# Fifteen whole output stores issued from SyncE's queue instead of ScalarE's, in a pruned-weight matrix product

## The chip, the cores and the metric

The kernel runs on one core of one Trainium2 chip. The metric is device microseconds (us) of one execution; the time before is 233.33 us, the median of three runs that lay between 233.15 and 233.38 us.

## What is computed

The reference takes x (16 x 512 x 1024, so 8192 rows of 1024 numbers in bf16), a weight w (1024 x 1024) and a bias b (1024). In every column of w, each group of four neighbouring rows keeps its two numbers of largest magnitude and the others become zero. The output is x times the pruned weight plus the bias.

```
wg = w.reshape(G, M, D)                    # M = 4, G = 256
mag = jnp.abs(wg)
order = jnp.argsort(mag, 1)
thr = jnp.take_along_axis(mag, order[:, M - N:M - N + 1, :], 1)     # N = 2
mask = mag >= thr
wp = (wg * mask).reshape(D, D)
return jnp.einsum("bsd,df->bsf", x, wp) + b
```

## The kernel before

The 8192 rows are cut into 64 tiles of 128 rows (`NT = 64`, tiles 0 to 63). One tile needs sixteen matrix products: eight blocks of 128 along the inner dimension (`KT = 8`) by two halves of 512 output columns (`FH = 512`). TensorE wants x with the inner dimension on the partitions, so x has to come transposed.

The work has two stages. In the first, the weight is loaded, pruned on VectorE and spread into `wp_nat`, while the first tiles are begun with what is there; its order is written out by hand, engine by engine, in `order` (line 258). Nothing of it is touched here. It is over when the tiles of `closes` (line 389) are done: tiles 0 to 11.

The second stage is the loop at line 437 over seven batches of tiles: tiles 12 to 15, and then six batches of eight, 16 to 23, 24 to 31, 32 to 39, 40 to 47, 48 to 55 and 56 to 63. A batch of x is brought by one transposing DMA, `load_nat` (line 374, the DMA at line 377), into a buffer `xb`, of which there are two (line 56). It is issued from SyncE's queue, SP. At the head of batch `bi` the program issues the load of batch `bi + 1` (line 439). With two buffers, that load may start when TensorE is through with batch `bi - 1`, and its data are needed when TensorE comes to batch `bi + 1`. So one load waits on SP for the last product of a batch and has the time of the next batch to land.

For each tile, TensorE makes its sixteen products into two banks `ps` of PSUM (`psum_o` has six, line 59); VectorE adds the bias to each half and writes it to `o` (`evac`, line 398, the instruction at line 400); and one DMA of 256 KB stores `o` to the output (`store`, line 411, which goes through `issue`, line 96). There are ten buffers `o` (line 57), so the buffer of one tile is written again ten tiles later.

A DMA is issued by an engine's queue: SP, which does no arithmetic, or ScalarE's queue, ACTq. ScalarE itself has nothing to compute in the second stage. Each queue works in the order in which the program issues, which `seq` (line 64) pins: an issue that waits holds up everything behind it in its queue. Within a batch the program order is: the load of the next batch, and then the eight stores.

From tile 59 on (`LATE = 5`), each tile is stored by halves, all from ACTq. The last tile, 63, is cut into four pieces, whose stores are issued in turn from SP and ACTq (line 449). Thus in the program before, SP issues nothing between the load of tiles 56 to 63 and the first piece of tile 63.

Of the kernel before, what the change touches and what calls it, by code (L numbers as in the profile page):

```python
# [10 lines left out]
def kernel(  # L11
# [20 lines left out]
    NT = NTOK // P  # L32
# [63 lines left out]
    def issue(eng, out_, in_):  # L96
        q = nc.sync if eng == "sp" else nc.scalar
        return seq(eng, q.dma_start(out_, in_))  # L98
# [138 lines left out]
    def nat(xt, ps, c0, c1, k0=0, k1=KT, first=0, last=KT - 1, koff=0):  # L237
        for kt in range(k0, k1):
            pe(nc.tensor.matmul(ps, lhsT=xt[:, kt - koff, :], rhs=wp_nat[:, kt, c0:c1],  # L239
                                start=(kt == first), stop=(kt == last)))  # L240
# [139 lines left out]
    def load_batch(bi):  # L380
        if bi < len(batches):
            tb, nb = batches[bi]
            xnat.update(load_nat(tb, tb + nb))
# [14 lines left out]
    def evac(o, ps, c0, c1, add=None):  # L398
        if add is None:
            dve(nc.vector.tensor_tensor(o[:, c0:c1], ps, bias_sb[:, c0:c1], op=Alu.add))  # L400
        else:
            dve(nc.vector.tensor_tensor(o[:, c0:c1].rearrange("p (n c) -> p n c", n=2),  # L402
                                        ps.rearrange("p (n c) -> p n c", n=2), add, op=Alu.add))

    def rows(t):
        if t < NPK:
            ov, n = tokens(of, t)
            return ov[:, n, :]
        return of[t * P:(t + 1) * P, :]

    def store(eng, t, o, c0=0, c1=Dout):
        issue(eng, rows(t)[:, c0:c1], o[:, c0:c1])
# [24 lines left out]
    for bi, (tb, nb) in enumerate(batches):  # L437
        if bi:
            load_batch(bi + 1)
        for j in range(nb):  # L440
            t = tb + j
            xt = xnat[t]
            o = outp.tile([P, Dout], bf16, name="o")
            if t == NT - 1:
                for n, (c0, c1) in enumerate(((0, FH), (FH, FH + CW), (FH + CW, Dout - P), (Dout - P, Dout))):
                    ps = psum_o.tile([P, FH], fp32, name="ps")
                    nat(xt, ps[:, :c1 - c0], c0, c1)
                    evac(o, ps[:, :c1 - c0], c0, c1)
                    store("act" if n % 2 else "sp", t, o, c0, c1)
            else:  # L450
                pss = [psum_o.tile([P, FH], fp32, name="ps") for _ in range(2)]
                for kt in range(KT):
                    for h in range(2):
                        nat(xt, pss[h][:], h * FH, (h + 1) * FH, kt, kt + 1)
                for h in range(2):
                    evac(o, pss[h][:], h * FH, (h + 1) * FH)
                    if t >= NT - LATE:
                        store("act", t, o, h * FH, (h + 1) * FH)
                if t < NT - LATE:
                    store("act", t, o)  # L460


# [28 lines left out]
```

## Time and profile before

| what | value |
|---|---|
| time, median of three runs | 233.33 us |
| time of the profiled execution | 233.28 us |
| its span, first to last instruction | 231.5 us |
| TensorE clock granted, mean | 1.000 |
| VectorE busy (L400 and L402 among it) | 108.1 us, 47% |
| ScalarE busy | 13.7 us, 6% |
| one load of eight tiles, at line 377, from issue to landing, median | 13.9 us |
| one store of 256 KB from ACTq, from issue to landing, median | 2.6 us |

The span is what the profile covers; 1.78 us of the profiled execution's time lie around it. Lines of the profile name an engine (PE is TensorE, DVE is VectorE, ACT is ScalarE, SP is SyncE; a q behind a name is that engine's queue of issues), a line of the kernel, and what is written from what: `o<-ps,bias_sb` is a tile `o` written from `ps` and `bias_sb`. A wait reads "waiter <- what it waited for". Where a DMA is issued, the duration is that of the issuing instruction on its queue; the time to landing is given separately.

### The profile page before, as it was taken

The numbers are of one execution on the slowest core, as the hardware profiler recorded it, in microseconds if no ns is written. First come the engines' busy times: TensorE is split into PE (matmuls) and PEld (weight loads), VectorE is DVE, ScalarE is ACT, GpSimd is POOL, SyncE is SP. The second block draws the span as 40 slices with busy tenths as digits, with TensorE's granted clock in tenths as the row PEclk, the third lists the DMA queues.
The fourth block names the chain that finished last, engine by engine and source line by source line (L and its number), as shares of the span: only waits on it lengthen the run. The fifth ranks groups of instructions, "written<-read, shape, count | busy, mean of one in ns | idle before, by whom it ended". The sixth has DMA issues, their size and how long they took to land.

```text
span 231.5 us, 2851 instructions
## 1 busy us (share of the span) xinstructions
PE 227.7 (98%) x1158; PEld 112.4 (49%) x1158; DVE 108.1 (47%) x188; ACT 13.7 (6%) x27; POOL 17.6 (8%) x15
## 2 busy tenths in 40 slices
PE   8999999999999999999999999999999999999995
PEld 4887444544444444444444444444444444444443
DVE  4999878854334324324424424424424423433434
ACT  3674100000000000000000000000000000000000
POOL 1000199700000000000000000000000000000000
PEclk9999999999999999999999999999999999999999
DMA  6989989996399221993259921695229952122122
GB/s 184 348 221 224 224 180 259 305 226 242 136 213 269 106 93 62 216 238 123 88 114 221 254 93 61 170 268 159 72 91 189 224 176 83 56 91 86 57 87 91
DMA packets 78268, 38.19 MB, mean 165 GB/s; under 512 B 63664, under 2 KB 70576, under 8 KB 78256
## 3 DMA queue, kind: packets, MB, share of 16 engines
q1 hardware_dynamic: 67328, 20.61, 44.3%
q10 hardware_dynamic: 10928, 17.40, 21.8%
q8 instruction: 9, 0.15, 0.3%
q14 instruction: 3, 0.02, 0.0%
HBM read 3.41 MB, written 16.78 MB: 87 GB/s over the span
## 4 chain that ended last, share of the span: by engine, by line
PE 96%; DVE 1%; DMA 1%; ACTq 0%; issue 0%
PE ps L239 88%; PE ps L216 6%; PE tp L239 1%; DMA w_sb<-in_w_dram 1%; PE tp L189 1%; DVE hi L154 0%; DVE lo L154 0%; DVE mag L154 0%; ACTq L98 0%; DVE mag L164 0%; DVE o L400 0%; DVE wp L154 0%
## 5 line engine op out<-in xcount | busy, mean ns | idle before, releaser
L239 PE MATMUL ps<-wp_nat,xb 128*128 128x512 bf16 (+2 forms) x848 | 179.8, 375 | 0.0
L239 PEld LDWEIGHTS <-xb 128*128 128x128 bf16 x848 | 82.4, 98 | 97.5
L400 DVE TENSOR_TENSOR o<-ps,bias_sb 128x512 bf16<-128x512 f32 (+1 forms) x112 | 71.6, 677 | 113.9 <-PE ps L239 113.8
L396 POOL TENSOR_TENSOR st<-st,bias_sb 128x1024 f32<-128x1024 f32 x8 | 16.7, 2131 | 0.0
L216 PE MATMUL ps<-wp,xt 128*128 128x256 bf16 x128 | 15.1, 273 | 0.1
L239 PE MATMUL ps<-wp_nat,xlow 128*128 128x512 bf16 x64 | 14.1, 379 | 0.0
L216 PEld LDWEIGHTS <-xt 128*128 128x128 bf16 x128 | 12.3, 98 | 1.7 <-ACT xt L194 0.2
L402 DVE TENSOR_TENSOR o<-ps,st 128x512 bf16<-128x512 f32 x16 | 11.1, 692 | 2.8 <-PE ps L239 2.3
L239 PE MATMUL ps<-wp_nat,xlead 128*128 128x512 bf16 x48 | 11.2, 379 | 0.0
L239 PEld LDWEIGHTS <-xlow 128*128 128x128 bf16 x64 | 7.2, 112 | 6.7
L239 PEld LDWEIGHTS <-xlead 128*128 128x128 bf16 x64 | 6.2, 98 | 7.1
L256 ACT COPY st<-ps 128x512 f32<-128x512 f32 x16 | 8.4, 595 | 6.5 <-PE ps L216 3.7
L154 DVE TENSOR_TENSOR mag<-mag,hi 128x256 bf16<-128x256 bf16 (+3 forms) x10 | 5.6, 583 | 0.2
L154 DVE TENSOR_TENSOR wp<-w_sb,mag 128x256 bf16<-128x256 bf16 (+3 forms) x10 | 5.6, 582 | 0.1
L133 PE MATMUL ps<-const-bfloat16-1.0 128*128 128x128 bf16 (+1 forms) x22 | 4.0, 364 | 0.8 <-PEq L475 0.8
L164 DVE TENSOR_SCALAR mag<-w_sb 128x512 uint16<-128x512 uint16 (+2 forms) x6 | 2.7, 469 | 3.2 <-DMA w_sb<-in_w_dram 3.2
L239 PE MATMUL tp<-wp_nat,xlead 128*128 128x512 bf16 x16 | 4.1, 379 | 0.0
L133 PEld LDWEIGHTS <-const-bfloat16-1.0 128*128 128x128 bf16 x22 | 2.2, 131 | 2.4 <-issue 2.4
L154 DVE TENSOR_TENSOR hi<-mag 128x512 bf16<-128x512 bf16 (+2 forms) x7 | 3.2, 459 | 0.1
L189 PE MATMUL tp<-ident,x 128*128 128x128 bf16 x32 | 3.0, 221 | 0.3 <-ACT xt L194 0.2
L154 DVE TENSOR_TENSOR lo<-mag 128x512 bf16<-128x512 bf16 (+2 forms) x7 | 3.2, 457 | 0.0
L194 ACT COPY xt<-tp 128x256 f32<-128x256 f32 x8 | 2.9, 374 | 3.2 <-PE tp L189 3.2
(15 smaller groups left out, 13.4 us busy)
## 6 DMA issues: line engine op xcount, KB each, us to landing
out_dram<-o ACTq DMA_DIRECT2D x59, 256.0 KB, 2.6
wp_nat<-wp SPq DMA_DIRECT2D x14, 128.0 KB, 3.5
w_sb<-in_w_dram SPq DMA_DIRECT2D x3, 512.0 KB, 7.0
out_dram<-o ACTq DMA_DIRECT2D x8, 128.0 KB, 1.7
x<-in_x_dram SPq DMA_DIRECT2D x2, 256.0 KB, 4.1
w_sb<-in_w_dram SPq DMA_DIRECT2D x1, 256.0 KB, 5.1
x<-in_x_dram ACTq DMA_DIRECT2D x1, 256.0 KB, 4.3
bias_sb<-in_b_dram SPq DMA_DIRECT2D x1, 256.0 KB, 7.1
```

Of the source, the lines that this page charges most:

```text
L133: pe(nc.tensor.matmul(warm_ps[:, :rep * P], lhsT=nc.const_aps.tensor(1.0, [P, P], bf16), rhs=nc.const_aps.tensor(1.0, [P, rep * P], bf16), ...
L154: dve(nc.vector.tensor_tensor(out, a, b_, op=op))
L164: dve(nc.vector.tensor_single_scalar(self.mag[:, ms, :].bitcast(u16), self.w[:, ms, :].bitcast(u16), 0x7FFF, op=Alu.bitwise_and))
L189: pe(nc.tensor.transpose(tp[:, m, :], xg[:, m, :], ident[:]))
L194: act(nc.scalar.copy(xt[:].bitcast(fp32), xpk[t].bitcast(fp32)))
L216: pe(nc.tensor.matmul(ps[:, c0 + d:c1 + d], lhsT=xpk[t][:, m, :], rhs=wp[:, g, m, c0:c1], start=(new and m == ms.start), stop=(left[(q, n) ...
L239: pe(nc.tensor.matmul(ps, lhsT=xt[:, kt - koff, :], rhs=wp_nat[:, kt, c0:c1], start=(kt == first), stop=(kt == last)))
L256: act(nc.scalar.copy(st[:, n % 2, :, :].rearrange("p t c -> p (t c)"), ps_open.pop((q, n))[:]))
L396: pool(nc.gpsimd.tensor_tensor(st[:], st[:], bias[:, :, None, :].to_broadcast([P, 2, 2, CW]), op=Alu.add))
L400: dve(nc.vector.tensor_tensor(o[:, c0:c1], ps, bias_sb[:, c0:c1], op=Alu.add))
L402: dve(nc.vector.tensor_tensor(o[:, c0:c1].rearrange("p (n c) -> p n c", n=2), ps.rearrange("p (n c) -> p n c", n=2), add, op=Alu.add))
```

## The change

The whole stores of the odd tiles from 29 to 57, fifteen in number, are issued from SP instead of ACTq. `NT - 36` is 28, and `NT - LATE` is 59. The even tiles, the tiles before 28, the half stores from tile 59 on and the pieces of tile 63 stay where they are, and no data, buffer or loop is changed.

```
                     if t >= NT - LATE:
                         store("act", t, o, h * FH, (h + 1) * FH)
                 if t < NT - LATE:
-                    store("act", t, o)
+                    store("sp" if t >= NT - 36 and t % 2 else "act", t, o)
```

Two of the moved stores (29 and 31) fall in the batch 24 to 31; four each fall in the batches 32 to 39, 40 to 47 and 48 to 55; one (57) falls in the last batch. The last tiles of these batches (31, 39, 47, 55) are odd, so the stores of 31, 39 and 47 stand on SP directly ahead of a load; behind that of 55 no load is left.

More of the change, by code (lines that the diff above doesn't have):

```diff
@@ L459 @@
                 if t < NT - LATE:
-                    store("act", t, o)
+                    store("sp" if t >= NT - 36 and t % 2 else "act", t, o)
 _INS = ['x', 'w', 'b']
```

## The prediction

> **What bounds the kernel now.** I read the page's busy time first, then the chain of waits, and then, because the edit touches only queues, the waits of SP's queue, the pace of VectorE and the issues and landings of the loads.
>
> ```profile
> PE 227.7 (98%) x1158; PEld 112.4 (49%) x1158; DVE 108.1 (47%) x188; ACT 13.7 (6%) x27; POOL 17.6 (8%) x15
> PE 96%; DVE 1%; DMA 1%; ACTq 0%; issue 0%
> ```
>
> ```profile
> 37.97 190.85 PE ps L239 x900
> 228.82 0.02 issue
> 228.85 0.29 DVE o L400
> ```
>
> The first line is the busy time: TensorE works 98% of the span. The others are the chain that ended last: from 37.97 us it is TensorE's products alone, 190.85 us without a step to another engine, then 0.29 us of VectorE's last addition. No store, no load and no queue appears in it in the part of the program that the edit touches, which begins with tile 29. So the time changes only if something makes TensorE wait after about 110 us, or if the 2.4 us behind the last addition (229.14 to 231.5) change.
>
> The timeline of VectorE gives TensorE's pace, since each pair of additions starts when TensorE has ended a tile:
>
> ```profile
> 118.08 1.29 DVE L400 TENSOR_TENSOR o<-ps,bias_sb 128x512 bf16<-128x512 f32 x2 [2.17 <-PE ps L239]
> 121.54 1.29 DVE L400 TENSOR_TENSOR o<-ps,bias_sb 128x512 bf16<-128x512 f32 x2 [2.16 <-PE ps L239]
> 124.99 1.29 DVE L400 TENSOR_TENSOR o<-ps,bias_sb 128x512 bf16<-128x512 f32 x2 [2.17 <-PE ps L239]
> ...
> 145.71 1.29 DVE L400 TENSOR_TENSOR o<-ps,bias_sb 128x512 bf16<-128x512 f32 x2 [2.16 <-PE ps L239]
> ```
>
> A tile takes 3.45 us (121.54 - 118.08 = 3.46; over eight tiles, (145.71 - 118.08) / 8 = 3.454). The first of these rows is tile 31: the load behind it starts 0.21 us later. The last is tile 39. A batch lasts 27.6 us.
>
> **SP before.** The issues of the three loads that will have moved stores ahead of them (the timeline of SP's queue), and what SP waits for:
>
> ```profile
> 118.29 9.85 SPq L377 DMA_TRANSPOSE xb<-in_x_dram  x1
> ...
> 145.92 8.81 SPq L377 DMA_TRANSPOSE xb<-in_x_dram  x1
> ...
> 173.55 10.07 SPq L377 DMA_TRANSPOSE xb<-in_x_dram  x1
> ```
>
> ```profile
> SPq L377 <- PE ps L239: 116.8, 5, 28.7
> SPq L98 <- DMA out_dram<-o: 33.6, 1, 33.6
> SPq L98 <- DVE o L400: 11.0, 2, 10.5
> ```
>
> Issuing a load occupies SP for about 10 us, and the rest of a batch (some 17 us) SP waits for TensorE. The load at 118.29 brings tiles 40 to 47, needed when tile 39 ends, at 145.71. The second wait shows that an issue waits for older DMAs too: the first piece of tile 63 waited 33.6 us, from the end of the load's issue (173.55 + 10.07 = 183.62) to 217.2, which is when the first half of tile 59 had landed, eight issues earlier (its addition began at 214.78 and took 0.69, the store 1.7 us).
>
> ```profile
> out_dram<-o ACTq DMA_DIRECT2D x59, 256.0 KB, 2.6
> xb<-in_x_dram SPq DMA_TRANSPOSE x7, 13.9
> out_dram<-o SPq DMA_DIRECT2D x1, 128.0 KB, 1.8
> ```
>
> These are issues with the time to landing. The three loads above, taken one by one, landed in 13.9, 13.1 and 14.0 us; the longest of all seven took 17.4.
>
> **The change, part by part.**
>
> *Off ACTq:* fifteen issues of 0.338 us (median of the 69 output stores there), 5.1 us of a queue that stands on no chain and whose engine computes nothing after 36 us. Worth nothing: TensorE's products cover it.
>
> *Onto SP, ahead of a load.* Before, the load at 118.29 went out 0.21 us after TensorE's last product of the batch. Now the store of tile 31 stands ahead of it and waits for VectorE: 118.08 + 1.29 = 119.37. Then come 0.03 us to the issue (SP's last-tile store went out at 227.80, its addition having ended at 227.08 + 0.69 = 227.77), 0.36 us for the issue (SP's two output stores took 344 and 368 ns), and some 0.05 us to the next. The load goes out at 119.8, **1.5 us late**. A whole store from SP is not in the trace; SP's copies took 0.34 to 1.57 us to issue, so the delay lies between 1.5 and 2.7 us. Should the load's packets also have to wait until the store has landed (up to 2.9 us, the median of the stores beside the load at 90.67), it is 5.6 at most; at least it is 1.3 (SP's waits gone, the store's issue at nothing). I take 1.5, because the nearest rows are SP's own output stores. This happens to three loads, 4.6 us in all, and costs nothing while each lands in time: 119.8 + 13.9 = 133.7 against 145.7, **12.0 us to spare**; the third, 175.1 + 14.0 = 189.1 against 200.96, leaves 11.9. At the worst of all bounds, 118.29 + 5.6 + 17.4 = 141.3, it is still 4.4 us early. Without that cover each late load would cost its delay.
>
> *Onto SP, behind a load.* The additions of tile 33 end at 124.99 + 1.29 = 126.28, but SP is then issuing the load until 119.8 + 9.85 = 129.65; this store goes out 3.4 us later than from ACTq. The other odd stores of the batch come after 129.65 and do not wait for SP. How long a store takes to land behind a transpose is bounded by 1.8 us (the SP store at the end, with nothing in front) and 17.4 us (as slow as the slowest load). The spreads of the weight on the same queue are near rows: four copies issued right behind the two transposes of `xlead` landed in 3.0 us, four in front of them in 3.9, so I take 3 us: tile 33 has landed by 132.7, at the latest by 147.1. Its buffer `o` is written again by tile 43, at 124.99 + 10 x 3.454 = 159.5, so 12 us remain even at the bound. The DMA eight issues later, which may wait for it, is the store of tile 40, at 149.16 + 1.29 = 150.5, and nothing on TensorE's side waits for that in turn for another ten tiles. The sum over this part is nothing; the work that hides it is ten tiles of products, 34.5 us.
>
> The page "DMA: Bandwidth & Descriptors" of the Trainium skill (section "Queues, rings and completion order") says that each DMA engine takes up the descriptors of one queue in the order they were put there, and that SP and ScalarE have a queue each. It speaks against the change: on SP the store of tile 33 would have to stand behind a whole batch of transposes, on ACTq it need not. By that rule the store lands only near the load's own end, about 134 us; by the copies of `wp_nat` in the trace at about 133; the total is the same by both, as 159.5 is far off.
>
> *The end.* Tile 57's additions end near 209.2 (207.87 + 1.29), SP is free then (the store of tile 55 goes out near 202.3), and its next issue, the first piece of tile 63, is at 227.80: eighteen us lie between. The last issue of all, from ACTq at 229.2, follows the last addition by 0.06 us. Nothing of it changes.
>
> **Sum.** 231.5 us of span + 0, and 1.78 us around it: 233.28, where the three runs have a median of 233.33. I predict **233.3 us**. The runs spread by 0.1%, and 0.2% (0.47 us) is about what this kernel's measurement can tell from no change.
>
> **The rivals.**
>
> *A load comes late (slower).* The loads and their stores now share one ordered queue, and mixing copies into transposes could stretch a load: its stretch of the trace is already full (DMA share 1.10 and 208 GB/s from 90.7 to 104.6 us, 0.26 and 96 GB/s in the rest of the batch). The place is the first product of tiles 40, 48 and 56. It decides once a load takes longer than 27.4 - 1.5 = 25.9 us to land, 1.9 times the 13.9 seen. At twice its time (27.8) it costs 1.9 us a batch, three times: 5.7, or 239.0 us. Against it: copies and transposes already alternate on SP between 10 and 35 us, and none there took over 17.4. Chance 0.05.
>
> *TensorE's pace falls a little (slower).* The edit puts other packets next to the products; 0.25% of the 118 us behind tile 29 is 0.3, 0.4% is 0.5: 233.8. Against it: the tile takes 3.45 us in the crowded half of a batch and in the quiet half alike. With other unseen fixed costs of this size, 0.10.
>
> *The tail gets shorter (faster).* Fewer issues on ACTq could let the end close sooner. SP's waits for the last stores sum to 1.4 us in the closing; half of that gone gives 232.6. Against it: the last eight stores from ACTq are the same ones, 3.45 us apart by pairs, and each lands in about 1.7. Chance 0.08.
>
> *The edit does not move what it says.* The condition holds for 15 tiles and SP can issue plain stores (two are in the trace); the time would be the same 233.3. It is counted with no change.
>
> **How the numbers follow.** No change: 0.77, faster 0.08, slower 0.15. The unknown costs all stay under their cover, so the likeliest case has its own range of 232.9 to 233.8. To leave out under 2 in 10, I stretch it to 232.7 and 234.3, which takes in part of the tail and the pace cases; the late load lies outside.
>
> **What would show it.** Section 6 should list 44 whole stores from ACTq and 15 from SP. The loads near 118.3, 145.9 and 173.6 should go out 1.5 us later, land in 13 to 17 us, and SP should wait for VectorE instead of TensorE there. The store of tile 33 should go out near 129.7. TensorE's pieces in the chain should stay unbroken from 38 to 228.8 us. The prediction is wrong if TensorE's chain breaks at tile 40, 48 or 56 for a DMA into `xb`, if VectorE waits for a DMA out of `o`, or if the span behind the last addition is not 2.4 us.

## The result, and the profile after

The changed kernel takes 233.77 us (median of 22 runs, 233.48 to 234.31), the kernel before, run beside it, 233.37 us (22 runs, 233.01 to 233.67). The ratio is 1.0017 with a 95% interval of 1.0011 to 1.0023: a loss of 0.4 us, small but clear of the spread. The profiled execution took 234.01 us, its span 232.2.

On the two queues the profile is as the prediction said, except that the loads land sooner than its 13 to 17 us. First the page's DMA issues of the kernel after (times to landing last), with the loads' line from its view of DMA queues:

```profile
out_dram<-o ACTq DMA_DIRECT2D x44, 256.0 KB, 2.8
out_dram<-o SPq DMA_DIRECT2D x15, 256.0 KB, 2.0
...
xb<-in_x_dram SPq DMA_TRANSPOSE x7, 11.2
```

Fifteen whole stores are on SP, and the median load lands sooner than before (11.2 against 13.9 us), not later. The timeline of SP's queue after the change, and VectorE's at the end of tile 31:

```profile
118.36 1.29 DVE L400 TENSOR_TENSOR o<-ps,bias_sb 128x512 bf16<-128x512 f32 x2 [2.17 <-PE ps L239]
```

```profile
112.77 7.24 SPq L98 DMA_DIRECT2D out_dram<-o  x2
120.11 8.54 SPq L377 DMA_TRANSPOSE xb<-in_x_dram  x1
128.74 18.90 SPq L98 DMA_DIRECT2D out_dram<-o  x4
147.73 8.98 SPq L377 DMA_TRANSPOSE xb<-in_x_dram  x1
```

The load goes out 1.75 us after tile 31's additions begin; before it was 0.21 (118.29 - 118.08). It is 1.54 us late. The end of the chain of waits shows that this costs nothing:

```profile
38.25 190.85 PE ps L239 x900
229.10 0.02 issue
229.13 0.29 DVE o L400
```

TensorE's last stretch is 190.85 us long, to the digit what it was. It begins 0.28 us later because this one execution was that late already near 10 us, long before any moved store: the chain's long piece of the first stage, 11.35 us on PE, begins at 10.06 us instead of 9.78. Three of the four other kernels below that lose time begin it between 9.77 and 9.85 us. So of the 0.75 us between the two spans, 0.28 belong to the start of this execution, and the rest stands behind the last addition. That stretch lasted 229.14 to 231.47 us, 2.33 us, before, and lasts 229.42 to 232.22, **2.80 us**, now.

The view of DMA from 227 us to the end, of the kernel before and of the kernel after (for queues: packets, MB, share of the 16 engines; for issues: size and time to landing):

```profile
out_dram<-o SPq DMA_DIRECT2D x1, 128.0 KB, 1.8
out_dram<-o ACTq DMA_DIRECT2D x1, 64.0 KB, 1.6
out_dram<-o SPq DMA_DIRECT2D x1, 32.0 KB, 1.5
out_dram<-o ACTq DMA_DIRECT2D x1, 32.0 KB, 1.5
```

```profile
q14 instruction: 1, 0.01, 0.5%
...
out_dram<-o SPq DMA_DIRECT2D x1, 128.0 KB, 1.7
out_dram<-o ACTq DMA_DIRECT2D x1, 64.0 KB, 2.3
out_dram<-o SPq DMA_DIRECT2D x1, 32.0 KB, 2.2
out_dram<-o ACTq DMA_DIRECT2D x1, 32.0 KB, 1.9
```

The last three pieces of tile 63 land 0.4 to 0.7 us later, and one packet is there that was not there before: a load of instructions, `q14 instruction`. In the trace it has 8192 bytes, starts at 229.78 us, 0.36 us behind the last addition, and takes 0.46 us. The page's list of queues says the same of the whole span: `q14 instruction` went from 3 packets to 4.

One more reading ties the packet to the stores. A store completes in sixteen parts, whose completions the trace records one by one. In us behind the last addition, for the very last piece (32 KB from ACTq), the first and the three last of the sixteen:

```
              first   14th   15th   16th
before         1.34   1.46   1.47   1.49
after          1.34   1.47   1.49   1.96
```

Fifteen parts land as before; one is 0.47 us late, as much as the tail (the stretch behind the last addition) is longer (2.80 - 2.33). Of each of the two pieces before it, too, one part of sixteen lands 0.6 to 0.7 us behind the other fifteen. The core has sixteen DMA engines; the trace does not name the one that carried the code load, but one part of sixteen held up is what one occupied engine would do. (The packets of `n14` below show it more closely.) SP's closing waits show where it is paid:

```profile
SPq L486 <- DMA out_dram<-o: 1.4, 4, 0.4
```

```profile
SPq L486 <- DMA out_dram<-o: 1.5, 2, 1.1
```

These are the waits at the end of the program, before and then after (sum, number, longest): the longest went from 0.4 to 1.1 us.

### The profile page after: what moved, and what is told of

The parts are those of the page before. It is cut to its first block, busy times and chain, and to the rows that moved or that the text cites. A ratio compares the mean times of both kernels' runs of the same rounds, so it can differ in the third digit from the quotient of the medians.

```text
span 232.2 us, 2851 instructions
## 1 busy us (share of the span) xinstructions
PE 228.3 (98%) x1158; PEld 113.0 (49%) x1158; DVE 108.0 (47%) x188; ACT 13.8 (6%) x27; POOL 17.6 (8%) x15
## 4 chain that ended last, share of the span: by engine, by line
PE 98%; DVE 0%; issue 0%
PE ps L239 88%; PE ps L216 6%; PE ps L133 2%; PE tp L239 1%; PE tp L189 1%; DVE o L400 0%
## 5 line engine op out<-in xcount | busy, mean ns | idle before, releaser
L239 PE MATMUL ps<-wp_nat,xlead 128*128 128x512 bf16 x48 | 11.2, 379 | 0.0
L189 PE MATMUL tp<-ident,x 128*128 128x128 bf16 x32 | 3.6, 252 | 0.0
(15 smaller groups left out, 13.9 us busy)
```

The costliest lines, as they stand in the source:

```text
L189: pe(nc.tensor.transpose(tp[:, m, :], xg[:, m, :], ident[:]))
```

## The experiments

Why is there a code load more? Each moved store puts two instructions on SP's queue, its issue and a wait for an older DMA, so SP has 90 instructions in the trace instead of 60. The theory (A): a queue fetches its code (its instructions) in blocks; SP comes to the end of one at about its 81st instruction, which now falls into the closing of the program. The rival (B): a store on SP's queue costs something by itself, through the loads it shares the queue with or through the pieces of tile 63 behind it. Theory A makes the loss depend only on how many instructions SP has and on when it comes to that one. Eight kernels were run, each 10 to 12 times, beside the kernel before.

**No store moved, thirty empty instructions on SP**

```
                     store("act", t, o)
+                    if t >= NT - 36 and t % 2:
+                        for _ in range(2):
+                            sp(nc.sync.drain())
```

> The kernel before, all stores from ACTq, with 30 empty instructions (drains) added to SP's queue in pairs behind the odd tiles 29 to 57; no DMA is moved. Theory A (a code load of 8 KB, started when SP comes to about its 81st instruction, falls among the last stores): SP has 90 instructions as after the change, so a code load of 8192 bytes appears 0.3 to 0.4 us behind the last addition, the last stores land 0.4 to 0.7 us later, the stretch from the last addition to the end of the span is 2.8 us instead of 2.33, and the time is 233.8, ratio 1.0017. Theory B (stores on SP's queue cost something by themselves, by sharing it with the loads or with the last pieces): no store is on SP, so 233.37 and a tail of 2.33 us.

Measured: 233.95 us, ratio 1.0020 (1.0011 to 1.0029). The view of DMA from 227 us on:

```profile
q14 instruction: 1, 0.01, 0.7%
...
out_dram<-o ACTq DMA_DIRECT2D x1, 64.0 KB, 2.5
out_dram<-o SPq DMA_DIRECT2D x1, 32.0 KB, 2.3
out_dram<-o ACTq DMA_DIRECT2D x1, 32.0 KB, 2.1
```

The whole loss without one moved DMA. The code load starts at 229.72, 0.26 us behind the last addition, and the tail is 2.94 us.

**Ten, twenty, and fifteen other stores moved**

```
-                    store("sp" if t >= NT - 36 and t % 2 else "act", t, o)
+                    store("sp" if t >= NT - 26 and t % 2 else "act", t, o)   # n10
+                    store("sp" if t >= 19 and t % 2 else "act", t, o)        # n20
+                    store("sp" if t <= 41 and t % 2 else "act", t, o)        # early15
```

> Ten stores moved instead of fifteen (odd tiles 39 to 57). Theory A: SP ends with 80 instructions, so no code load falls in the tail, which is 2.33 us; 233.4, ratio 1.000. Theory B: two thirds of the loss, 233.64, ratio 1.0011, with a tail between.

Measured: 233.36 us, ratio 1.000, with a wide interval (0.9983 to 1.0016; one of the twelve runs took 235.48 us); the tail is 2.39 us. By the time alone B's 1.0011 isn't excluded; by the trace the code load starts at 232.24, when the span is over, and the last three pieces land in 1.6, 1.5 and 1.5 us, as before.

> Twenty stores moved (odd tiles 19 to 57). Theory A: SP has 100 instructions and comes to its 81st some ten instructions earlier, at 185 to 200 us, so the code load stands in the middle of a batch where nothing waits for it; tail 2.33 us, 233.4, ratio 1.000. Theory B: four thirds of the loss, 233.9, ratio 1.0023.

Measured: 233.37 us, ratio 0.9997 (0.9987 to 1.0007); the code load starts at 186.3 and the tail is 2.33 us. More stores on SP than the change has, and no loss: B falls.

> Fifteen stores moved, but those of the odd tiles 13 to 41. Theory A: the number of SP's instructions is that of the change, so the code load is again in the tail: 2.8 us, 233.8, ratio 1.0017. Theory B in the form that the late stores or loads are to blame: nothing is moved behind tile 41, the tail is 2.33 us and the time 233.4.

Measured: 233.92 us, ratio 1.0021 (1.0012 to 1.0031); the code load starts at 229.48, and the tail is 2.69 us. So here it does not matter which stores are moved, late ones or early ones. This execution's last addition ended at 229.19, so it has the loss without the late start of the profiled execution above.

**One store fewer, one store more.** The trace of `n20` narrowed the place: the code load came while SP's 80th instruction still waited, 1.46 us after the 79th (184.84). In the changed kernel the 79th is at 228.46, 1.32 us ahead of its code load.

```
+                    store("sp" if t >= 31 and t % 2 else "act", t, o)        # n14
+                    store("sp" if t >= 27 and t % 2 else "act", t, o)        # n16
```

> Fourteen stores moved (odd tiles 31 to 57). In the runs so far the code load started 1.1 to 1.5 us after SP's 79th instruction. Theory A with that: here the 79th is the first wait of the closing, about 0.25 us behind the last issue from SP, so the code load starts 1.2 to 1.4 us behind the last addition, when the last pieces' data are being written or just have been: loss between 0 and 0.2 us, ratio 1.000 to 1.001, tail 2.33 to 2.5 us. Theory B (a cost per store on SP): 14/15 of the loss, ratio 1.0016.

Measured: 234.12 us (233.1 to 234.93), ratio 1.0032 (1.0018 to 1.0046), worse than the change. Here the expectation failed in size: it gave a loss of 0.2 us at most and a tail of 2.5. Three of the twelve runs, at 233.10 to 233.42 us, show no loss; their traces are not on record. The view of DMA from 227 us on:

```profile
q14 instruction: 1, 0.01, 0.6%
...
out_dram<-o ACTq DMA_DIRECT2D x1, 64.0 KB, 1.6
out_dram<-o SPq DMA_DIRECT2D x1, 32.0 KB, 1.5
out_dram<-o ACTq DMA_DIRECT2D x1, 32.0 KB, 2.3
```

The code load started at 230.19, earlier than reckoned (1.06 us behind the last addition and 1.1 behind the 79th instruction), and met the last piece alone. The trace has each packet: the last piece goes out as sixteen groups of nine packets. The packets of fifteen groups go out between 0.88 and 1.14 us behind the last addition; the nine of the sixteenth start at 1.64, where the code load ends (1.063 + 0.576 = 1.639). So one group stood behind the code load. Fifteen of its parts landed by 1.55, the sixteenth at 2.28; the tail is 3.12 us. That part is 0.79 us late, more than the 0.58 us of the code load; what the remaining 0.2 us are is not shown.

> Sixteen stores moved (odd tiles 27 to 57), one more than the change. Theory A: the 79th instruction is the one behind the store of tile 57, at about 217.5 us, so the code load starts near 219, ten us before the last addition; tail 2.33 us, 233.4, ratio 1.000. Theory B: 16/15 of the loss, ratio 1.0018.

Measured: 233.30 us, ratio 0.9998 (0.9990 to 1.0007). The code load starts at 218.65, the tail is 2.32 us, and the last piece lands in 1.5 us:

```profile
out_dram<-o SPq DMA_DIRECT2D x1, 128.0 KB, 1.7
out_dram<-o ACTq DMA_DIRECT2D x1, 64.0 KB, 1.6
out_dram<-o SPq DMA_DIRECT2D x1, 32.0 KB, 1.5
out_dram<-o ACTq DMA_DIRECT2D x1, 32.0 KB, 1.5
```

So by the medians, with ten stores moved there is no loss, with fourteen 0.8 us, with fifteen 0.4, with sixteen and twenty none. No cost per store behaves like that.

**The change, cured by more instructions**

```
                     store("sp" if t >= NT - 36 and t % 2 else "act", t, o)
+                    if t >= NT - 36 and t < NT - 26:
+                        sp(nc.sync.drain())
```

> The changed kernel with ten empty instructions (drains) added to SP's queue; the same fifteen stores are moved. Theory A: more instructions cure it, since SP comes to its 79th ten instructions earlier, at about 185 us: tail 2.33 us, 233.4, ratio 1.000. Theory B: 233.8 or more, ratio 1.0017 or more.

Measured: 233.25 us, ratio 0.9999 (0.9991 to 1.0008); the code load starts at 186.43, the tail is 2.32 us, and the last two pieces land as in the kernel before:

```profile
out_dram<-o SPq DMA_DIRECT2D x1, 32.0 KB, 1.5
out_dram<-o ACTq DMA_DIRECT2D x1, 32.0 KB, 1.5
```

The fifteen stores of the change are moved, ten empty instructions are added, and the loss is gone.

**The same on ScalarE's queue**

```
                     store("act", t, o)
+                    if t >= NT - 36 and t < NT - 17:
+                        act(nc.scalar.drain())
```

> The kernel before with nineteen empty instructions (drains) added to ScalarE's queue, nothing else. VectorE's and ScalarE's first code loads started at their 63rd or 64th instruction, VectorE's second 128 later. Theory A, if it holds for any engine: ScalarE's 191st instruction falls at about 228.4 us, so a code load of 8192 bytes starts 0.2 to 0.8 us behind the last addition and the tail is 2.6 to 2.9 us; ratio 1.0015 to 1.002. If the cost were peculiar to SP's queue: no code load or no loss, 233.4.

Measured: 234.04 us, ratio 1.0030 (1.0021 to 1.0039). The loss is larger than was expected. A code load starts at 230.01, 0.80 us behind the last addition and 1.52 behind ScalarE's 191st instruction; the tail is 2.94 us. The view of DMA from 227 us on:

```profile
q14 instruction: 1, 0.01, 0.4%
...
out_dram<-o ACTq DMA_DIRECT2D x1, 64.0 KB, 1.6
out_dram<-o SPq DMA_DIRECT2D x1, 32.0 KB, 2.4
out_dram<-o ACTq DMA_DIRECT2D x1, 32.0 KB, 2.1
```

So the loss is not peculiar to SP's queue. (The count in the expectation is a little narrow: in the ten traces, 63 to 67 of ScalarE's instructions had begun when its first code load in the span started.)

In all five kernels that lose time, the changed one among them, exactly one of the sixteen parts of the last piece is late: it lands 1.85 to 2.28 us behind the last addition, against 1.49 in the kernel before, and the span ends 0.83 to 0.84 us behind it in each of them, as it does in the kernel before. So the late part is the whole loss of the traced executions. How late it is does not follow from the code load's length alone: 0.36 us late with a code load of 0.51 us (`early15`), 0.62 with one of 0.34 (`padact19`). None of the versions beats the kernel before beyond the spread; `n16`, `n20` and `afterpad10` equal it.

## Why the prediction failed, step by step

The time lies in the predicted range, and 0.17% is under the 0.2% that the text took for no change; but with 22 runs on each side it is a loss, and its cause was not among the steps.

- *What bounds the kernel*: right. TensorE's stretch is unbroken and of the same length, and so the time could change only in it or in the tail. It changed in the tail.
- *Onto SP, ahead of a load*: right. Predicted 1.5 us late, measured 1.54; hidden.
- *Onto SP, behind a load*: right, with a size off. The store of tile 33 was to go out at 129.65, which is 129.93 with this execution's late start; it went out at 128.74, as the load's issue took 8.5 us instead of 9.85, and landed in 2.8 us, where 3 was taken.
- *The rule on one queue's order* from the Trainium skill (page "DMA: Bandwidth & Descriptors", section "Queues, rings and completion order") put that landing near the load's own end. The load landed at 120.11 + 10.9 = 131.0, the store at about 131.5, so this row fits the rule as well as it fits the estimate of 3 us; nothing depended on it.
- *The end*: this is the step that failed. It put the change behind the last addition at nothing; that stretch went from 2.33 to 2.80 us, which was also the last of the prediction's own signs of being wrong. "Nothing of it changes" was reckoned from the order of DMAs and from what SP waits for, and not from SP's instructions as such. The step "Onto SP, ahead of a load" counted the time of the store's issue and left out that thirty instructions lengthen SP's code, which brings its next code load into the closing. The profile page of the kernel before had a sign of such loads in its list of queues (`q14 instruction: 3`), and the trace showed such packets of 8192 bytes at 29.6, 58.8 and 157.9 us, where no one waits.
- *The rivals*: the late load did not come, the loads were even faster. "TensorE's pace falls a little" gave 233.8, near the time measured, but that is luck, since the profile excludes its reason: the pace is the same to the digit. The rival on the tail had its place right and its sign wrong.

The page "Runtime: NRT & Kernel Launch" of the Trainium skill (section "Instruction fetch mechanics") says that code is brought in 16 KiB blocks of 256 instructions through a DMA queue that the engine's sequencer (the part that issues its instructions) drives while the current block runs, and that crossing a block's end is mostly hidden. TensorE's blocks fit (16384 bytes about every 27.6 us, a batch of 128 products and as many weight loads). The other engines' loads do not: here they have 8192 bytes, and the two that go with VectorE by its count of instructions come about 128 instructions apart. Hidden they are too, except for those that fell among the last stores, at a cost of 0.4 to 0.8 us.

## What to carry to other kernels

Moving or adding a cheap instruction also shifts the places where its queue fetches code, and such a fetch is itself a DMA (0.31 to 0.65 us for 8192 bytes in these traces, but for one of 1.95 us). In the middle it cost nothing that these runs can tell; among the last stores it cost 0.4 to 0.8 us. So for a change of a few tenths of a microsecond compare the count of instruction packets and the stretch behind the last computation before explaining anything else. A loss of this kind says nothing against the edit itself: with one store more, or with ten empty instructions, it was gone.

## What the runs showed of the hardware that was not expected

- The code load started 1.1 to 1.46 us after the start of SP's 79th recorded instruction in all eight kernels that had one for SP, the changed one among them (228.46 and 229.78 there; 184.84 and 186.3 in `n20`; 231.13 and 232.24 in `n10`).
- Loads of x landed sooner when the odd stores of a batch were behind them on the same queue: 10.9, 11.2 and 10.8 us, against 13.9, 13.1 and 14.0 for the same three loads before. With thirty empty instructions and no store moved (`pad30`) the median of all seven loads was 13.4 us, so it goes with the stores and not with the number of instructions. Fewer stores then ran beside the load from the other queue; whether that is what shortens it was not tried. It is worth nothing here, as each load had 12 us to spare before.
